# Two costs in a list scheduler: a longer tail for accumulating DMAs, a longer hop between engines

## The chip, the cores and the metric

The kernel runs on one core of a Trainium2 chip. The core has five engines that work through their own instruction queues in fixed order and meet only at semaphores: TensorE (PE, matmuls), VectorE (DVE), ScalarE (ACT), GpSimd (POOL, here memsets and four DMAs) and SyncE (SP, which issues the loads and stores). The metric is the device time of one execution in microseconds (us). A profile is one execution taken by the hardware profiler; its rows give starts and lengths in us from the start of the span.

## The reference

The reference is the joint network of a speech model. Inputs are bf16; B = 2, T = 4000, D = 512, K = 5 taps, U = 8.

```python
xp = jnp.pad(x, ((0,0),(pad,pad),(0,0)))
h = sum of einsum("btc,cd->btd", xp[:, i:i+T, :], w1[i]) over the 5 taps
h = gelu(h)[:, ::2, :]                      # (2, 2000, 512)
f = the same with hp = pad(h) and w2
f = gelu(f)[:, ::2, :]                      # (2, 1000, 512)
fe = einsum("btd,de->bte", f, w_f)
ge = einsum("bud,de->bue", g, w_g)
j = tanh(fe[:, :, None, :] + ge[:, None, :, :])
return einsum("btud,dv->btuv", j, w_o)      # (2, 1000, 8, 512)
```

So there are two convolutions of stride 2, a projection, a tanh over every pair of time and label, and a last matmul over 16000 rows.

## The kernel before, in words

**Layout.** Channels lie on the partitions, 512 channels as 4 blocks of 128: `k` numbers the blocks of a product's input, `m` those of its output. The program's batch 0 is `x[1]`, and its batch 1 is `x[0]`.

**Convolutions.** A convolution of stride 2 is done with fewer products than taps: sums and differences of inputs (on VectorE) are multiplied with sums and differences of weights (VectorE and ScalarE), and the results are recombined. Batch 0's first convolution runs in three tiles of columns (`Tile_`, L628), two of 252 columns per phase and one of 498. For each tile and each `m`, `stages` gives five pieces: `one` and `two` (products, a copy to `cs` on ScalarE, a subtraction `acc<-cs,acc` on VectorE), then `end0` and `end1`, eight matmuls each, followed by a gelu on ScalarE into `hT` (L650). The second convolution of batch 0 and both of batch 1 use `Triple` (L705), which makes three output phases from six input phases. `prepare(k0, k1)` builds its operands on VectorE from `hT` or `zx`: float32 intermediates `q` in `r32b` or `r32` (operations of 336 columns a block, 672 for two blocks), the operands `t0`, `ti`, `t1`, `tm`, `s1`, `sm` in `wide` or `row`, and `s0`, `si`, `t2` in place. `stages` then does the products, with copies to `sd` on ScalarE. For batch 0, `prepare` is called for input blocks 0 and 1 together, then for block 2, then for block 3; the products of `s1` and `t1` over blocks 0 to 2 stand ahead of those over block 3 (`split`, L770). A `tail_zero` memset on VectorE (L994, shown at L996) comes before each `prepare` and waits for the gelus that write the blocks concerned.

**Weights for the second convolution.** `w2sums` (L598) builds sums and differences. `w2quads` (L610) needs `4*w2[4] + 2*w2[2] + w2[0]` and lets DMAs add: ScalarE writes `4*w2[4]` as float32 into `half` (two buffers, `half0` and `half1`, each for two output blocks) and `2*w2[2]` into `w2_t[1]`, POOL issues two accumulating DMAs for each half (`acc`, L589, issue at L590), and ScalarE converts `half` back into `w2_t[1]` with a scale of 1/3. That last conversion, `w_t<-half`, waits for the second accumulation.

```python
act(v, w2_sb[4, :, sl], ACT.Copy, scale=4.0)
act(t, w2_sb[2, :, sl], ACT.Copy, scale=2.0)
acc(v, w2_sb[0, :, sl])
acc(v, t)
act(t, v, ACT.Copy, scale=1.0 / 3.0)
```

`w1extra` (L619) builds further first-layer weights for batch 1 by four `quad` calls: two multiplies on VectorE through the buffers `ws32_0` to `ws32_3` (shown as `ws`) and a copy on ScalarE (`w_sb<-ws`).

**Loads.** SP loads the first weights and inputs, then the second layer's weights. The six transposing loads of `zx0` (batch 1's input) have a dependency on the last accumulating DMA (`load_z`, L469).

**Joint part.** `fe` (L972) projects batch 0, with twelve copies to `feT` on VectorE or ScalarE. `tanh` (L983) writes `jT` in rings of 2048 columns for each `k`. `joint_tile` (L1007) multiplies 128 rows with `wo_sb`, evacuates the bank to `ost` on VectorE or ScalarE, and SP stores it. The 125 tiles are placed between batch 1's convolutions, and the rest follow at the end.

**What sets the order.** Nothing runs when it is written down. All calls make entries in a `Plan` (L67), with a cost each. `edges` (L100) finds the dependencies. `schedule` (L144) computes a latest start for each entry backwards and runs `simulate` (L190) up to 16 times; each time `urge` (L172) makes the entries before TensorE's gaps more urgent, and the order with the shortest simulated end is kept. In `simulate`, TensorE and SP take the first ready entry in program order; ScalarE, VectorE and POOL take the one with the earliest latest start. A dependency that needs a semaphore adds `HOP`; a DMA issued by POOL ends by a formula for a queue with a bandwidth and a fixed tail. Up to `pl.pin = ()` some engines are pinned to program order (all four until `pl.pin = ("pe",)`, then TensorE alone). `emit` (L236) writes each engine's queue in the order found, with the semaphore waits.

Of the kernel before, what the change touches and what calls it, by code (L numbers as in the profile page):

```python
# [66 lines left out]
class Plan:  # L67


    COMPUTE = ("pe", "act", "dve", "pool")  # L70
    HOP = 0.16
    ROUNDS = 16

    def __init__(self, nc):
# [69 lines left out]
    def schedule(self, pred):  # L144


        ops, HOP = self.ops, self.HOP
        n = len(ops)
# [5 lines left out]
        for i in range(n - 1, -1, -1):  # L154
            o = ops[i]
            span = o.cost + ((8.0 if o.eng == "pool" else 4.0) if o.dma else 0.0)
            t = min([late[s] - (HOP if pred[s][i] else o.cost - span) for s in succ[i]], default=0.0)
            if o.eng == "pe":
# [31 lines left out]
    def simulate(self, pred, succ, late):  # L190


        ops, HOP = self.ops, self.HOP
        n = len(ops)
        left = [len(p) for p in pred]
        ready = [0.0] * n
        free = {e: 0.0 for e in ("pe", "act", "dve", "pool", "sp")}
        cand = {e: [] for e in free}
        for i in range(n):
            if not left[i]:  # L200
                cand[ops[i].eng].append(i)
        order = {e: [] for e in free}
        wire, soft, start = 0.0, 0.0, [0.0] * n
        for _ in range(n):
            best = None
            for e, c in cand.items():
                if c:
                    t = max(free[e], min([ready[i] for i in c]))
                    if best is None or t < best[0]:
                        best = (t, e)  # L210
            t, e = best
            now = [i for i in cand[e] if ready[i] <= t + 0.02]
            i = min(now) if e in ("pe", "sp") else min(now, key=lambda i: (late[i], i))
            cand[e].remove(i)
            order[e].append(i)
            o = ops[i]
            start[i] = t
            free[e] = t + o.cost
            end = free[e]
            if o.dma and e == "pool":  # L220
                soft = max(soft, end + 1.0)
                busy = wire > soft + 1.0
                soft += o.nbytes / (60e3 if busy else 230e3)
                wire += o.nbytes / 220e3 if busy else 0.0
                end = max(soft, end + 2.0)
            elif o.dma:
                wire = max(wire, t + 1.3) + o.nbytes / o.rate
                end = max(wire, t + 2.0)
            for s in succ[i]:
                ready[s] = max(ready[s], end + HOP if pred[s][i] else free[e])  # L230
                left[s] -= 1
                if not left[s]:
                    cand[ops[s].eng].append(s)
        return order, start, max(free.values())
# [902 lines left out]
```

## Time and profile before

Median of 11 runs: 269.83 us (269.01 to 270.21).

| What | us |
|---|---|
| the profiled execution's own time | 269.4 |
| its span, first to last instruction | 267.6 |
| TensorE busy in the span | 259.8 (97%) |
| VectorE busy | 201.1 (75%) |
| ScalarE busy | 181.1 (68%) |
| POOL busy | 6.9 (3%) |
| TensorE idle before its first matmul (1.19) and waiting for `wide` (1.74) and `jT` (0.70) | 3.6 |
| first matmul of the second convolution of batch 0 | starts at 59.20 |
| first matmul of a joint tile | starts at 90.29 |

The granted TensorE clock is 1.0 of full speed over the span. A timeline row reads: start, length, engine, line, operation, output and input tiles, shapes, how many, and in brackets how long the engine stood idle before and what ended it. Several rows of one kind in succession are merged, and consecutive operations of an engine overlap by some 0.08 to 0.1 us, so that the step from start to start is a little less than the length. Rows of a helper carry the helper's line (L404 and L585 on VectorE, L409 on ScalarE, L417 on TensorE); the tile names tell them apart. The chain of waits follows the work that ended last back to the start.

### The profile page before, as it was taken

What the parts mean: (1) busy time and instruction counts of PE and PEld (TensorE: products, weight loads), DVE (VectorE), ACT (ScalarE), POOL (GpSimd) and SP (SyncE); (2) the same over time, 40 slices, a digit from 0 to 9 for tenths busy, and PEclk for the clock granted to TensorE, in tenths of its full rate; (3) what the DMA queues carried; (4) which work ended last, traced back from release to release, by engine and by line L of the source; (5) the groups of instructions that cost most, each with busy time, mean ns of one, the idle gap of its engine ahead of it and who ended that gap; (6) DMA issues with size and microseconds to landing.
All of it is one profiled execution on the core that took longest, in us unless ns stands there. A gap on an engine that the chain in (4) does not pass through costs nothing.

```text
span 267.6 us, 4331 instructions
## 1 busy us (share of the span) xinstructions
PE 259.8 (97%) x1582; PEld 151.9 (57%) x1582; DVE 201.1 (75%) x362; ACT 181.1 (68%) x302; POOL 6.9 (3%) x20
## 2 busy tenths in 40 slices
PE   8999999979999899999999999999999999999995
PEld 4897854436666555655655555565565444444442
DVE  1999999889999999994424999743255666666654
ACT  2878969684366999658448488548447695959720
POOL 1000005100000000000000000000000000000000
PEclk9999999999999999999999999999999999999999
DMA  7999998979993022111111214312101443554444
GB/s 247 319 175 211 309 236 154 161 129 191 218 178 66 13 93 72 60 40 60 43 56 42 78 40 138 120 59 78 42 20 60 148 149 118 174 178 160 154 145 132
DMA packets 56706, 33.91 MB, mean 127 GB/s; under 512 B 31582, under 2 KB 56430, under 8 KB 56686
## 3 DMA queue, kind: packets, MB, share of 16 engines
q1 hardware_dynamic: 54430, 31.49, 44.4%
q0 software_dynamic: 2112, 2.10, 4.5%
q8 instruction: 12, 0.20, 0.3%
q14 instruction: 8, 0.07, 0.1%
q10 hardware_dynamic: 144, 0.07, 0.1%
HBM read 7.86 MB, written 16.38 MB: 91 GB/s over the span
## 4 chain that ended last, share of the span: by engine, by line
PE 70%; DVE 19%; DMA 5%; issue 3%; ACT 3%; DVEq 0%; ACTq 0%
PE acc L417 70%; DMA w_sb<-in_w_dram 4%; DVE wide L404 2%; DVE r L585 2%; DVE w_t L585 2%; DVE r32b L585 2%; DVE ws L404 2%; DMA xr<-in_x_dram 1%; DVE hT L404 1%; DVE ws L585 1%; ACT jT L409 1%; DVE w_sb L404 1%; DVE feT L981 1%; DVE w_t L404 1%; DVE sd L585 1%
## 5 line engine op out<-in xcount | busy, mean ns | idle before, releaser
L417 PE MATMUL acc<-wo_sb,jT 128*128 128x512 bf16 (+1 forms) x504 | 114.9, 377 | 0.7 <-ACT jT L409 0.7
L1029 DVE CAST ost<-acc 128x512 bf16<-128x512 f32 (+1 forms) x95 | 64.9, 688 | 37.9 <-PE acc L417 36.7
L409 ACT ACTIVATE jT<-feT,geT 128x1000 bf16<-128x1000 f32 (+16 forms) x100 | 76.5, 819 | 13.4 <-PE acc L417 10.3
L417 PEld LDWEIGHTS acc<-wo_sb,jT 128*128 128x128 bf16 x504 | 49.2, 98 | 53.5 <-ACT jT L409 1.0
L409 ACT ACTIVATE ost<-acc 128x512 bf16<-128x512 f32 (+1 forms) x31 | 18.0, 582 | 15.9 <-PE acc L417 15.6
L417 PE MATMUL acc<-xt,w_sb 128*128 128x252 bf16 (+1 forms) x144 | 23.5, 305 | 0.0
L409 ACT ACTIVATE hT<-acc 128x334 bf16<-128x334 f32 (+3 forms) x33 | 15.1, 463 | 9.6 <-PE acc L417 9.5
L409 ACT ACTIVATE sd<-acc 128x334 f32<-128x334 f32 (+1 forms) x32 | 13.8, 443 | 11.0 <-PE acc L417 11.0
L417 PE MATMUL acc<-row,w_sb 128*128 128x334 bf16 (+1 forms) x112 | 20.5, 305 | 0.0
L417 PEld LDWEIGHTS acc<-xt,w_sb 128*128 128x128 bf16 x144 | 14.1, 98 | 6.7
L417 PE MATMUL acc<-zx,w_sb 128*128 128x334 bf16 (+1 forms) x96 | 17.6, 305 | 0.0
L404 DVE TENSOR_TENSOR sd<-sd 128x334 f32<-128x334 f32 (+1 forms) x16 | 8.1, 504 | 10.8 <-ACT sd L409 10.7
L417 PE MATMUL acc<-row,w_t 128*128 128x334 bf16 (+1 forms) x80 | 14.6, 305 | 0.0
L417 PEld LDWEIGHTS acc<-row,w_sb 128*128 128x128 bf16 x112 | 10.9, 98 | 6.2
L417 PE MATMUL acc<-xs,w_t 128*128 128x252 bf16 (+1 forms) x76 | 14.0, 314 | 0.3 <-ACT cs L409 0.2
L417 PE MATMUL acc<-fT,wf_sb 128*128 128x333 bf16 (+1 forms) x96 | 14.0, 305 | 0.2 <-ACT fT L409 0.2
L409 ACT ACTIVATE fT<-acc 128x334 bf16<-128x334 f32 (+1 forms) x16 | 7.1, 446 | 8.0 <-PE acc L417 7.7
L417 PEld LDWEIGHTS acc<-zx,w_sb 128*128 128x128 bf16 x96 | 9.4, 98 | 5.4
L417 PEld LDWEIGHTS acc<-fT,wf_sb 128*128 128x128 bf16 x96 | 9.3, 97 | 4.5 <-ACT fT L409 0.2
L417 PE MATMUL acc<-xs,w_sb 128*128 128x252 bf16 (+1 forms) x72 | 11.4, 293 | 0.4 <-issue 0.4
L417 PE MATMUL acc<-hT,w_t 128*128 128x334 bf16 x64 | 11.7, 305 | 0.0
L417 PE MATMUL acc<-hT,w_sb 128*128 128x334 bf16 x64 | 11.5, 305 | 0.0
(86 smaller groups left out, 318.8 us busy)
## 6 DMA issues: line engine op xcount, KB each, us to landing
out_dram<-ost SPq DMA_DIRECT2D x109, 128.0 KB, 1.9
w_sb<-in_w_dram SPq DMA_DIRECT2D x10, 512.0 KB, 5.6
xr<-in_x_dram SPq DMA_DIRECT2D x2, 512.0 KB, 4.0
half<-w_sb POOLq DMA_DIRECT2D x2, 512.0 KB, 6.6
half<-w_t POOLq DMA_DIRECT2D x2, 512.0 KB, 5.4
wf_sb<-in_w_f_dram SPq DMA_DIRECT2D x1, 512.0 KB, 7.6
wg_sb<-in_w_g_dram SPq DMA_DIRECT2D x1, 512.0 KB, 6.3
wo_sb<-in_w_o_dram SPq DMA_DIRECT2D x1, 512.0 KB, 7.1
```

Of the source, the lines that this page charges most:

```text
L404: pl.op(eng, lambda e: e.tensor_tensor(out=o.ap, in0=a.ap, in1=b.ap, op=op), (a, b), (o,), vec_cost(o, (a, b)))
L409: pl.op("act", lambda e: e.activation(o.ap, i.ap, func, scale=scale, bias=0.0 if bias is None else bias.ap), rd, (o,), cost or o.ap.free_s ...
L417: ins = e.matmul(o.ap, lhsT=l.ap, rhs=r.ap, start=start and n == 0, stop=stop and n == len(pairs) - 1, skip_group_check=not check)
L585: pl.op(eng, lambda e: e.scalar_tensor_tensor(out=o.ap, in0=a.ap, scalar=f, in1=b.ap, op0=ALU.mult, op1=op), (a, b), (o,), vec_cost(o, (a, ...
L981: pl.op("dve", lambda e, o=o, v=v: e.tensor_copy(out=o.ap, in_=v.ap), (v,), (o,), 0.47)
L1029: pl.op("dve", lambda e, o=o, v=v: e.tensor_copy(out=o.ap, in_=v.ap), (v,), (o,), vec_cost(o, (v,)))
```

## The change

`HOP`, which `schedule` and `simulate` add to a dependency across engines, becomes 0.2 where it was 0.16. In `simulate`, a DMA issued by POOL begins to move data 3.0 after its issue has ended where it was 1.0, and ends at the earliest 4.0 after the issue where it was 2.0. Nothing else in the program is altered; the operations are the same, and the planner puts them into another order. SP's and POOL's queues come out in the same order as before. On ScalarE and VectorE entries change places between 18 and 120 us of the old trace and at a few places between 150 and 170; on TensorE the products of the second convolution of batch 0 do.

```diff
@@ class Plan
-    HOP = 0.16
+    HOP = 0.2
@@ simulate
             if o.dma and e == "pool":
-                soft = max(soft, end + 1.0)
+                soft = max(soft, end + 3.0)
                 busy = wire > soft + 1.0
                 soft += o.nbytes / (60e3 if busy else 230e3)
                 wire += o.nbytes / 220e3 if busy else 0.0
-                end = max(soft, end + 2.0)
+                end = max(soft, end + 4.0)
```

ScalarE's list around the accumulated weights, before and after (hT<-acc are the gelus of the 498-column tile, b.1 its first for block b and b.2 its second):

```diff
 hT<-acc 1.1 (block 1, first)
-w_sb<-w_sb
-w_t<-half0
-hT<-acc 1.2
-w_sb<-ws
-w_t<-half1
-hT<-acc 2.1
-w_t<-w_t
-w_sb<-ws
-hT<-acc 2.2
-hT<-hT (blocks 0, 1)
-w_t<-w_t
-hT<-acc 3.1
-hT<-hT (block 2)
-hT<-acc 3.2
+w_sb<-w_sb
+w_t<-w_t
+hT<-acc 1.2
+w_sb<-ws
+w_sb<-ws
+w_t<-w_t
+w_sb<-ws
+hT<-acc 2.1
+w_t<-half0
+hT<-acc 2.2
+hT<-hT (blocks 0, 1)
+w_t<-half1
+hT<-acc 3.1
+hT<-hT (block 2)
+hT<-acc 3.2
```

## The prediction

> **What bounds the kernel now.** I read the page's totals first, then TensorE's own waits, then the chain of work in order of time, then the timelines of ScalarE, VectorE and TensorE where that chain has holes.
>
> Page, busy shares and the chain by engine:
>
> ```profile
> span 267.6 us, 4331 instructions
> PE 259.8 (97%) x1582; PEld 151.9 (57%) x1582; DVE 201.1 (75%) x362; ACT 181.1 (68%) x302; POOL 6.9 (3%) x20
> ...
> PE 70%; DVE 19%; DMA 5%; issue 3%; ACT 3%; DVEq 0%; ACTq 0%
> ```
>
> TensorE is busy for 259.8 of 267.6 us, and the change alters no matmul. All it can win is TensorE's idle time, and all it can lose is new idle time. Where that idle time lies (us in total, times, longest):
>
> ```profile
> PE acc L417 <- DVE wide L404: 1.7, 1, 1.7
> ...
> PE acc L417 <- ACT jT L409: 0.7, 1, 0.7
> ```
>
> The rest of it is the start (1.2), three pieces of 0.2 to 0.4, and the last store. The chain in order of time (start, length, what):
>
> ```profile
> 51.69 0.96 issue
> ...
> 56.46 0.76 issue
> ...
> 90.29 174.02 PE acc L417 x968
> ```
>
> From 90.29 on TensorE waits for nothing. Before that, from 36.9 to 86.9, the chain runs along VectorE, with two holes in which VectorE itself stood. ScalarE's timeline says why (start, length, instruction, idle before it):
>
> ```profile
> 51.06 1.06 ACT L409 ACTIVATE w_t<-half 128x1024 bf16<-128x1024 f32 x1 [1.68 <-DMA half<-w_t]
> 52.03 0.57 ACT L409 ACTIVATE hT<-acc 128x498 bf16<-128x498 f32 x1
> ...
> 54.13 1.06 ACT L409 ACTIVATE w_t<-half 128x1024 bf16<-128x1024 f32 x1 [1.01 <-DMA half<-w_t]
> 55.09 0.57 ACT L409 ACTIVATE hT<-acc 128x498 bf16<-128x498 f32 x1
> ...
> 56.59 0.58 ACT L409 ACTIVATE hT<-acc 128x498 bf16<-128x498 f32 x1
> ```
>
> ScalarE reached the two conversions of the accumulated weights (half0, half1) before the accumulating DMAs had landed, and stood 1.68 and 1.01 us. The gelus (hT<-acc) queued behind. A gelu can start 0.20 after its products end (block 0's second gelu: products to 43.86, start 44.06). Block 1's second one was ready at 49.95 and ran at 52.03; block 2's second was ready at 54.15 and ran at 56.59. VectorE's preparation of the second convolution waits for exactly these two, first in its memsets:
>
> ```profile
> 52.64 0.68 DVE L585 SCALAR_TENSOR_TENSOR ws<-w_sb 128x512 f32<-128x512 bf16 x1 [0.97 <-DVE acc L404]
> ...
> 57.22 0.84 DVE L404 TENSOR_TENSOR wide<-r32b 128x668 bf16<-128x668 f32 x1 [0.76 <-issue]
> ```
>
> TensorE then comes to the end of the first convolution with nothing prepared:
>
> ```profile
> 56.46 1.00 PE L417 MATMUL acc<-xt,w_sb 128*128 128x498 bf16 x4
> 59.20 0.60 PE L417 MATMUL acc<-wide,w_t 128*128 128x334 bf16 x3 [1.74 <-DVE wide L404]
> ```
>
> **The change part by part.** It changes two costs in the planner; what the chip sees is the new order in each queue, which I read from the instruction lists of both kernels. No compute instruction or DMA is added or removed. POOL's queue and SP's queue keep their order. The steps:
>
> *1. ScalarE, 38 to 58 us.* The conversion of half0 moves behind block 2's first gelu, that of half1 behind block 2's second; three copies of the extra first-layer weights fill the space. Walk with lengths from the rows (gelu 0.46, weight copy 0.52, conversion 0.97, copy of 668 columns 0.65, each start to start): block 1's second gelu 49.95 to 50.4, copies to 52.0, a fourth copy to 52.8, block 2's first gelu (ready 52.45) to 53.2, half0 to 54.2, block 2's second gelu (ready 54.15) to 54.7, the hT copy to 55.3, half1 to 56.3, block 3's first gelu to 56.8, its second (ready 57.5) to 58.1. The accumulations landed by 51.06 and 54.13; the reads now stand at 53.2 and 55.3, so 2.1 and 1.2 us are in hand. Queued behind these reads are block 2's second and block 3's first gelu; the latter is 0.5 late, and VectorE comes to its memset for block 3 only at 59.1. The use of the converted weights is at 66.01 in the old trace (hT,w_t matmuls), far behind.
>
> *2. VectorE, 51 to 64 us.* The memset that waited to 52.60 now needs a gelu that ends at 50.4; VectorE is there at 51.6 (last acc at 51.00, 0.60 long). The weight multiply in this place is another one of the same 0.60. So the first 672-column operation starts at 52.25 where it started at 53.24: 0.99 won. Two of these at 0.77, then 0.41, 0.77, 0.42: 55.4. The memset for block 2 needs the gelu of 54.7: no hole, 0.76 won. Then 0.76 to 56.15, and the planner has put the 334-column sum (wide<-hT, 0.24) for block 2 ahead of its two 0.42 operations: it is ready at 56.4. Further 0.42, 0.42, 0.24, 0.42: the t1 operand at 57.9; then 0.42, 0.77, three of 0.42, 0.24 and 0.42: block 3's two operands at 60.6 and 61.0 (before: 62.0 and 62.4). VectorE is 0.99 + 0.76 = 1.75 ahead.
>
> *3. TensorE, 57 to 64 us.* It ends the first convolution at 57.30 and finds s1 of blocks 0 to 2 there (56.4). Its list now takes s1 for two output blocks (2 x 0.43) ahead of t1, needed at 58.15, there at 57.9. At 60.7 it needs block 3's s1 (60.6), at 61.13 t1 (61.0). These are tight; with a copy of the finished sums to sd that now starts 0.28 later relative to the matmuls I allow up to 0.3 of new waits. TensorE is 1.6 to 1.9 ahead from here.
>
> *4. From 64 to 90.29.* VectorE is busy without a hole here, and the swaps (one r32 operation before the sd pair of block 3, one zx operation before the first feT copy, the same operations in each sum up to the feT copy at 84.63) do not lengthen its queue before that copy. The tanhs follow: at 85.26 ScalarE starts on them and is busy to 90.2, in the same list but for one 0.41 tanh ahead of a feT copy. So the first joint tile's tanh comes 1.75 earlier. TensorE arrives 1.6 to 1.9 earlier and still waits 0.5 to 0.8 there, as now 0.70.
>
> *5. The zx loads.* SP starts them when the last accumulation lands (54.16 in the old trace); POOL's order is kept, and the half0 copy on ScalarE moves ahead of one gelu (up to 0.8 earlier), so they do not come later. Each issue takes 1.75; the third ends at 59.4, landing took at most 9.3, so at most 68.7, and VectorE wants them at 73.95 - 1.75 = 72.2. Hidden; with that cover gone each us of lateness would cost one.
>
> *6. The first 25 us.* A copy to tc moves behind a long shift on ScalarE (1.77), so the copy to cs, for which TensorE waited 0.19 at 24.74, comes 0.27 earlier; on VectorE one 0.60 operation passes another. Bounds: -0.33 (both small holes there gone) to +0.60 (one operation late); I take 0, nearest to the swap of equals.
>
> *7. After 90.29.* Swaps of evacuations with zx, row and jT operations, and one 0.60 weight multiply of block 3 that was done at 52.64 and is now done near 112, against another that left 95.03. The trace shows no TensorE wait here, so it does not show how much slack there is. Bounds: 0 to one VectorE operation (0.77) at each of two or three places; I take 0, since the idle time of ScalarE before its evacuations (15.6 us in 13 waits) and VectorE's (36.7 in 68) says that evacuation mostly waits for TensorE, not the reverse.
>
> Sum: -1.75. The profiled execution took 269.4 (span 267.6 and 1.8 around it), which gives 267.65; it lies 0.43 under the median of 269.83, so the forecast against the median is **268.1**.
>
> A rule that speaks against step 1: the accumulating DMA issued by POOL at 45.15 was seen as landed at 51.06 (5.9 us), the one at 49.26 at 54.13 (4.9). The Trainium skill, "DMA: Bandwidth & Descriptors", section "Anatomy of one DMA — SWDGE (gpsimd) path", puts such a transfer at about 2.0 us plus bytes / 436e3, an estimate of 3.2 us for 512 KB. By that figure the third would land at 48.35, before ScalarE stands free at 49.38, and later reads would win nothing there (269.8 in all). The row decides against the rule.
>
> **The rivals.** (a) *Given back at the first joint tile*: if tanh does not move with VectorE, the wait at 90.29 grows from 0.70 by what was won, and the time is 269.8. For it: TensorE waits there now. Against: the chain leads from that wait through feT copies into VectorE's gapless queue. (b) *Half of it*: the accumulations land later in the new order, or block 3's operands come late; one of the two holes stays (0.99 or 0.76), 268.9. (c) *More*: the wait for jT goes too, and the small ones: 1.74 + 0.70 + 0.16 = 2.6, 267.2. Against: both ends of it move alike. (d) *Slower*: between 91 and 121 VectorE is full, and the new list puts zx (0.41), r32 (0.77), row (0.77) and the 0.60 multiply ahead of evacuations whose banks TensorE takes next. Together 2.55 if none has slack: 269.83 - 1.75 + 2.55 = 270.6. It decides from 1.75 of them on. Against: TensorE never waited for a bank there, and in the same stretch one 0.60 operation is gone. (e) *The planner did not do what its costs say*: excluded by the lists, where both reads have moved.
>
> **How the numbers follow.** A difference under 0.2% (0.54 us) can't be told from none. Forecast near 268.1 (0.3 either way): 0.62. (b): 0.13. (c): 0.09. (a): 0.08. (d): 0.08. Faster by over 0.2%: 0.62 + 0.13 + 0.09 = 0.84; same 0.08; slower 0.08. The range takes in (c) at its lower end, and above (b) one further operation of 0.5: 267.2 to 269.4; what it leaves out is (a) and (d), 0.16.
>
> **What would show it.** Right: the conversions of half without idle time for a DMA; block 2's second gelu near 54.2; VectorE's first 672-column operation near 52.2, no hole at 56; TensorE's 1.7 wait for wide gone or under 0.4; the first jT matmul near 88.5, then none idle. Wrong: conversions still waiting; an unchanged time of the first joint tile (a); TensorE idle between 90 and 125 for an evacuation or sd (d).

## The result and the profile after

The changed kernel took 267.75 us (median; 267.33 to 268.20), beside 269.45 us for the kernel before on the same chip (median; 268.58 to 270.39). The ratio, which is that of the mean times, is 0.9935, with a 95% interval of 0.9925 to 0.9946: faster by 0.65%, or 1.75 us (the medians differ by 1.70). The forecast was 268.1 us against the earlier median of 269.83, a ratio of 0.9936. Beside the experiments the changed kernel was run once more, on a chip with the kernel before at 269.77: 267.77 us, ratio 0.9924 [0.9906, 0.9941].

The profiled execution took 267.66 us; its span is 265.9 where it was 267.6. The page's totals and the chain's shares by engine:

```profile
span 265.9 us, 4332 instructions
PE 260.4 (98%) x1582; PEld 151.7 (57%) x1582; DVE 201.0 (76%) x362; ACT 181.3 (68%) x302; POOL 6.8 (3%) x20
...
PE 80%; DVE 14%; ACT 3%; issue 2%; DVEq 0%; ACTq 0%
```

The engines do the same work as before; what is gone is idle time of TensorE. The chain's shares do not show the change: the DMA's 5% before were the first loads, between 0.7 and 14.0 us, in whose place the chain now follows TensorE's own work. TensorE's own waits (us in total, times, longest) no longer hold the 1.7 for `wide`:

```profile
PE acc L417 <- DVE zero L424: 1.2, 1, 1.2
PE acc L417 <- ACT jT L409: 0.5, 1, 0.5
PE acc L417 <- issue: 0.3, 1, 0.3
PE acc L417 <- ACT fT L409: 0.2, 1, 0.2
```

ScalarE's timeline (start, length, instruction) where the accumulated weights are read. Neither conversion has a bracket for a DMA behind it any more, and the gelus at 52.99 and 54.40 (block 2's two) stand around the first one instead of behind both:

```profile
52.99 0.57 ACT L409 ACTIVATE hT<-acc 128x498 bf16<-128x498 f32 x1
53.45 1.05 ACT L409 ACTIVATE w_t<-half 128x1024 bf16<-128x1024 f32 x1
54.40 0.58 ACT L409 ACTIVATE hT<-acc 128x498 bf16<-128x498 f32 x1
...
55.51 1.06 ACT L409 ACTIVATE w_t<-half 128x1024 bf16<-128x1024 f32 x1
56.46 0.58 ACT L409 ACTIVATE hT<-acc 128x498 bf16<-128x498 f32 x1
```

VectorE's timeline: both holes (0.97 and 0.76) are filled. The first 672-column operation starts at 52.34 where it started at 53.24, and the sum that started at 57.22 starts at 55.48 without idle time:

```profile
52.34 1.61 DVE L585 SCALAR_TENSOR_TENSOR r32b<-hT 128x672 f32<-128x672 bf16 x2
...
55.48 0.84 DVE L404 TENSOR_TENSOR wide<-r32b 128x668 bf16<-128x668 f32 x1
```

TensorE's timeline: the first products on `wide` follow the last ones of the first convolution at once, and the first joint tile comes at 88.55 (before: 90.29). From there the chain of waits has one line, as it had before, of the same length:

```profile
56.70 1.00 PE L417 MATMUL acc<-xt,w_sb 128*128 128x498 bf16 x4
57.54 1.01 PE L417 MATMUL acc<-wide,w_t 128*128 128x334 bf16 x6
...
88.55 1.90 PE L417 MATMUL acc<-wo_sb,jT 128*128 128x512 bf16 x8 [0.47 <-ACT jT L409]
```

```profile
88.55 174.02 PE acc L417 x968
```

**A ruler for all runs.** Profiles of one kernel differ by some tenths before 30 us, so spans alone do not compare orders well. I cut each profile's span in three by two starts on TensorE's timeline, and show that profile's S, A and R beside the times of all runs: S is the start of the first 498-column matmul (the third tile of the first convolution); A goes from there to the first `fT` matmul, and holds the whole stretch around the accumulated weights; R is the rest. S + A + R is the span, which the page gives to 0.1, so R holds to about 0.05.

| Kernel | time, us | ratio to before [95%] | S | A | R |
|---|---|---|---|---|---|
| before | 269.45 | 1 | 29.91 | 50.42 | 187.27 |
| after | 267.75 | 0.9935 [0.9925, 0.9946] | 30.15 | 48.67 | 187.08 |
| after, again | 267.77 | 0.9924 [0.9906, 0.9941] | 30.06 | 48.67 | 187.07 |
| 1: two conversions moved | 268.65 | 0.9959 [0.9946, 0.9971] | 30.39 | 49.12 | 187.39 |
| 2: two conversions moved back | 268.28 | 0.9946 [0.9927, 0.9964] | 30.29 | 49.27 | 187.04 |
| 3: tail alone | 268.13 | 0.9942 [0.9919, 0.9964] | 29.94 | 48.56 | 187.30 |
| 4: hop alone | 268.58 | 0.9959 [0.9943, 0.9976] | 30.30 | 49.27 | 186.93 |
| 5: no second accumulation | 268.33 | 0.9940 [0.9918, 0.9962] | 30.68 | 48.56 | 187.26 |
| 6: orders of TensorE and VectorE alone | 269.81 | 0.9997 [0.9986, 1.0007] | 30.58 | 50.42 | 187.10 |
| 7: half copies earlier | 267.85 | 0.9931 [0.9915, 0.9948] | 30.78 | 48.56 | 187.26 |
| 8: tail of 5 | 268.04 | 0.9928 [0.9910, 0.9945] | 29.82 | 48.67 | 187.01 |
| 9: short tanhs first, on after | 267.95 | 0.9924 [0.9912, 0.9936] | 29.93 | 48.66 | 187.11 |
| 10: the same, on the tail alone | 267.92 | 0.9932 [0.9914, 0.9949] | 29.88 | 48.56 | 187.36 |
| 11: and two more tanhs, on after | 268.26 | 0.9942 [0.9922, 0.9962] | 30.72 | 48.67 | 187.11 |

### The profile page after: what moved, and what is told of

Read it like the earlier page. It is cut to its first block, busy times and chain, and to the rows that moved or that the text cites. A ratio compares the mean times of both kernels' runs of the same rounds, so it can differ in the third digit from the quotient of the medians.

```text
span 265.9 us, 4332 instructions
## 1 busy us (share of the span) xinstructions
PE 260.4 (98%) x1582; PEld 151.7 (57%) x1582; DVE 201.0 (76%) x362; ACT 181.3 (68%) x302; POOL 6.8 (3%) x20
## 4 chain that ended last, share of the span: by engine, by line
PE 80%; DVE 14%; ACT 3%; issue 2%; DVEq 0%; ACTq 0%
PE acc L417 79%; DVE wide L404 2%; DVE r L585 2%; DVE r32b L585 2%; ACT w_t L409 1%; DVE ws L585 1%; DVE hT L404 1%; ACT jT L409 1%; DVE feT L981 1%; PE acc L510 1%; DVE sd L585 1%; DVE wide L734 1%; DVE row L585 1%; DVE row L734 1%; DVE acc L585 1%
```

## The experiments

Theory A, the prediction's: ScalarE reaches the conversions before the accumulating DMAs have landed and stands; the gelus queued behind are late, and through them VectorE and TensorE. Theory B: the conversions' wait is only where it shows, and the gain comes from the order of other work, above all TensorE's `s1` ahead of `t1` and VectorE's early sum for block 2. The diffs are lists of instructions in shortened form, ScalarE's unless said otherwise; g2.1 is block 2's first gelu. "Counted from S" means less that profile's S.

**1 and 2. The two conversions alone, forwards and back.** In the order of before, only the two conversions move:

```diff
 g1.1
-w_t<-half0
 g1.2
 w_sb<-ws
-w_t<-half1
 g2.1
+w_t<-half0
 w_t<-w_t
 w_sb<-ws
 g2.2
+w_t<-half1
```

> The order of before, with two entries of ScalarE's queue moved and nothing else: the conversion of half0 goes behind block 2's first gelu, that of half1 behind block 2's second. Theory A (ScalarE's queue stood for the accumulating DMAs, and the gelus behind it held VectorE): VectorE's holes of 0.97 and 0.76 go, TensorE's wait for wide falls from 1.74 to under 0.3, ratio to before 0.9925 to 0.9950, some 267.5 to 268.1 us. Theory B (the won time comes from the other moves: s1 of two output blocks ahead of t1 on TensorE, the block 2 sum ahead of its 336-column operations on VectorE): none of these is made here, so 0.998 to 1.002.

Measured: 0.9959 [0.9946, 0.9971], between the two ranges: less than theory A gave, more than theory B. ScalarE has no DMA wait left, and the list of TensorE's waits names no matmul that waited for `wide` (two of its weight loads still do, 0.8 together): A falls from 50.42 to 49.12, by 1.30 of the 1.75 that the change wins there. Something is still late, and ScalarE's and VectorE's timelines name it:

```profile
53.43 1.05 ACT L409 ACTIVATE w_t<-half 128x1024 bf16<-128x1024 f32 x1
54.37 0.62 ACT L409 ACTIVATE w_t<-w_t 128x512 bf16<-128x512 bf16 x1
54.89 0.62 ACT L409 ACTIVATE w_sb<-ws 128x512 bf16<-128x512 f32 x1
55.41 0.57 ACT L409 ACTIVATE hT<-acc 128x498 bf16<-128x498 f32 x1
```

```profile
59.46 0.85 DVE L585 SCALAR_TENSOR_TENSOR r32b<-hT 128x672 f32<-128x672 bf16 x1 [0.43 <-issue]
```

g2.2 runs at 55.41, behind two weight copies that the changed kernel does earlier, in the time ScalarE used to stand; g3.2 and VectorE's operation on block 3 are late in the same way. So in this order the place of the conversions is the larger part. That the copies pulled into the gap are the rest of it is argued from these rows; the copies alone were not moved.

The other way round, the order of after with the two conversions put back ahead of the gelus:

```diff
 w_t<-w_t
+w_t<-half0
 g1.2
 w_sb<-ws
 w_sb<-ws
 w_t<-w_t
 w_sb<-ws
+w_t<-half1
 g2.1
-w_t<-half0
 g2.2
 hT<-hT
-w_t<-half1
```

> The order of after, with the same two conversions moved back ahead of the gelus they stood ahead of (half0 ahead of block 1's second, half1 ahead of block 2's first). Theory A: ScalarE waits for the accumulations again, 1.2 to 1.7 and 0.7 to 1.2 us, VectorE's holes return, and most of 1.7 us is given back, less up to 0.5 for the moves that stay: ratio to before 0.997 to 1.001. Theory B: the won time stays, ratio 0.993 to 0.995.

Measured: 0.9946 [0.9927, 0.9964], so theory A's number was missed and B's was hit. The reason is on ScalarE's timeline, where the conversions stand in the old places and still do not wait, and on POOL's, where the last two accumulations are issued 0.5 and 0.8 earlier than before (45.15 and 49.26), or 0.9 and 1.2 counted from S:

```profile
50.33 1.06 ACT L409 ACTIVATE w_t<-half 128x1024 bf16<-128x1024 f32 x1
51.29 0.57 ACT L409 ACTIVATE hT<-acc 128x498 bf16<-128x498 f32 x1
...
53.84 1.04 ACT L409 ACTIVATE w_t<-half 128x1024 bf16<-128x1024 f32 x1
54.78 1.05 ACT L409 ACTIVATE hT<-acc 128x498 bf16<-128x498 f32 x2
```

```profile
44.65 1.27 POOL L590 DMA_DIRECT2D half<-w_t  x1 [2.59 <-ACT w_t L409]
48.47 1.28 POOL L590 DMA_DIRECT2D half<-w_t  x1 [2.55 <-DMA half<-w_sb]
```

The rest of after's order had covered the wait already: ScalarE makes the two `half` copies one gelu earlier, and it has one more weight copy ahead of the first conversion than before, and three more ahead of the second. What moving back costs is 0.60 in A (49.27 against 48.67). VectorE's timeline shows where. Its memset at 51.98, which waits for block 1's second gelu, comes no later than in after (21.69 in both, counted from S). The weight multiply behind it waits for ScalarE's copy `w_sb<-ws`, which now stands behind the first conversion:

```profile
52.48 0.69 DVE L585 SCALAR_TENSOR_TENSOR ws<-w_sb,ws 128x512 f32<-128x512 bf16 x1 [0.43 <-ACT w_sb L409]
```

The first 672-column operation then comes 0.61 later than in after, counted from S. So work behind a conversion can be held in other ways than through the gelus. This run could not tell A from B, since both old DMA waits were gone; 3, 5 and 7 do.

**3 and 4. The two constants apart.** The tail alone, with the hop at 0.16; and the hop alone, with the old tail.

```diff
 # 3
     HOP = 0.16
-                soft = max(soft, end + 1.0)
+                soft = max(soft, end + 3.0)
-                end = max(soft, end + 2.0)
+                end = max(soft, end + 4.0)
```

> Only the tail of the accumulating DMAs is longer (3.0 and 4.0), the hop stays at 0.16. TensorE's order comes out as before; ScalarE's conversions move behind the gelus. Theory A: all of it, ratio 0.992 to 0.995, with TensorE's wait for wide under 0.3. Theory B: TensorE's order is as before and the block 2 sum stays behind its operations, so 0.998 to 1.002.

Measured: 0.9942 [0.9919, 0.9964]. TensorE's list is that of before, `s1` and `t1` in the old order, and yet there is no wait for `wide`; the conversions are read without waiting:

```profile
53.49 1.05 ACT L409 ACTIVATE w_t<-half 128x1024 bf16<-128x1024 f32 x1
54.44 0.58 ACT L409 ACTIVATE hT<-acc 128x498 bf16<-128x498 f32 x1
...
55.55 1.05 ACT L409 ACTIVATE w_t<-half 128x1024 bf16<-128x1024 f32 x1
```

A is 48.56, the least of all. TensorE's swap and VectorE's early sum are not needed for the gain in A.

```diff
 # 4
-    HOP = 0.16
+    HOP = 0.2
```

> Only the hop is longer (0.2), the tail as before. Both conversions stay ahead of block 1's second and block 2's first gelu; s1 is moved ahead as in the whole change, and other entries move. Theory A: ScalarE still waits 1.0 to 1.7 twice, VectorE keeps its holes, ratio 0.997 to 1.003. Theory B: ratio 0.993 to 0.996.

Measured: 0.9959 [0.9943, 0.9976]; A's expectation of no change was missed, and B's range was hit. The conversions keep their places and still wait, 1.02 and 0.98 in place of 1.68 and 1.01, but they start at 50.29 and 53.32 where they started at 51.06 and 54.13:

```profile
50.29 1.06 ACT L409 ACTIVATE w_t<-half 128x1024 bf16<-128x1024 f32 x1 [1.02 <-DMA half<-w_t]
51.25 0.57 ACT L409 ACTIVATE hT<-acc 128x498 bf16<-128x498 f32 x1
...
53.32 1.06 ACT L409 ACTIVATE w_t<-half 128x1024 bf16<-128x1024 f32 x1 [0.98 <-DMA half<-w_t]
```

The accumulations are issued at 44.67 and 48.45, as in 2. Counted from S, the conversions start 1.16 and 1.20 earlier than before. So the hop has another road to a gain of 1.15 in A: it does not read the sums later, it makes them earlier. VectorE's and TensorE's lists change in this kernel too (VectorE's first hole is filled with another multiply, its second is still 0.66), so how much of the 1.15 is due to the earlier sums alone is not separated here. The hop wins 0.34 more in R. The two constants' gains overlap and do not add: 1.86 and 1.15 apart, 1.75 together.

**5. The landing without the order.** The order of before on every engine, less two DMAs:

```diff
             acc(v, w2_sb[0, :, sl])
-            acc(v, t)
             act(t, v, ACT.Copy, scale=1.0 / 3.0)
```

> The order of before on every engine, with the second accumulating DMA of each half left out (the two that add 2*w2[2]), so that the sum of weights lacks that term; ScalarE's conversion of half0 then waits for a sum issued at about 39.8 us and landed near 45, that of half1 for one landed near 49, both ahead of their turns at 49.4 and about 51.5. Theory A (the late landing is the cause: ScalarE stands 1.7 and 1.0 us at the conversions, its gelus and through them VectorE and TensorE come late): no idle for a DMA ahead of the conversions, first gelu of block 2 at 53 to 54 where it began at 55.09, TensorE's wait for wide under 0.5 us where it was 1.74, ratio 0.992 to 0.997. Theory B (the order in which the pieces of work stand is what costs; the DMA's wait is only seen there): order unchanged, so ratio 0.999 to 1.001 and the wait for wide still 1.2 or more.

Measured: 0.9940 [0.9918, 0.9962]. With the sums there in time, the old order has no wait at the conversions, and the gelus follow them at 51.01 and 53.23:

```profile
50.06 1.05 ACT L409 ACTIVATE w_t<-half 128x1024 bf16<-128x1024 f32 x1
51.01 0.58 ACT L409 ACTIVATE hT<-acc 128x498 bf16<-128x498 f32 x1
...
51.99 1.06 ACT L409 ACTIVATE w_t<-half 128x1024 bf16<-128x1024 f32 x1
53.23 0.59 ACT L409 ACTIVATE hT<-acc 128x498 bf16<-128x498 f32 x1 [0.18 <-PE acc L417]
```

A is 48.56, as with the tail alone. Theory B, which wanted no change here, falls. This kernel also lets SP start the `zx` loads sooner (49.68), but VectorE takes them at 72.86 without idle time, as in all kernels here, and in 3, where the loads start at 54.26, A is the same.

**6. The other order without the landing.** ScalarE's list of before, with the lists of TensorE and VectorE that the changed planner makes:

```diff
 (in words)
-order = old plan on every engine
+order = old plan on ScalarE, new plan on TensorE and VectorE
```

> TensorE's and VectorE's orders are those of after, ScalarE's order is that of before, conversions and half copies in their old places. Theory A: ScalarE still stands about 1.7 and 1.0 us at the two conversions, so the gelus of blocks 1 and 2 keep their times within 0.4 us; products of s1 put ahead of t1 can shorten TensorE's wait for wide by some of 1.74 us, but the products and the fT evacuations behind them come no earlier, so ratio 0.997 to 1.002. Theory B: the orders of TensorE and VectorE carry the gain, ratio 0.993 to 0.996.

Measured: 0.9997 [0.9986, 1.0007], nothing. ScalarE stands at the conversions (1.13 and 1.01), and TensorE waits in two pieces, 0.70 and 0.47, where it waited 1.74 in one. The first `wide` product comes a little sooner and the next ones later, and A is 50.42, the same as before to the hundredth:

```profile
51.54 1.06 ACT L409 ACTIVATE w_t<-half 128x1024 bf16<-128x1024 f32 x1 [1.13 <-DMA half<-w_t]
...
54.60 1.06 ACT L409 ACTIVATE w_t<-half 128x1024 bf16<-128x1024 f32 x1 [1.01 <-DMA half<-w_t]
```

```profile
58.83 1.02 PE L417 MATMUL acc<-wide,w_t 128*128 128x334 bf16 x6 [0.70 <-DVE wide L404]
60.33 1.02 PE L417 MATMUL acc<-wide,w_sb 128*128 128x334 bf16 x6 [0.47 <-DVE wide L734]
```

VectorE's new list does not suit ScalarE's old one. Its memset waits for a gelu, as theory A has it, and then its multiply waits for a ScalarE copy that stands later in the old list:

```profile
53.16 0.07 DVE L996 MEMSET hT<- 128x8 bf16 x1 [0.48 <-ACT hT L409]
53.69 0.69 DVE L585 SCALAR_TENSOR_TENSOR ws<-w_sb,ws 128x512 f32<-128x512 bf16 x1 [0.46 <-ACT w_sb L409]
```

So the two lists of after bring nothing while ScalarE keeps its own. That they would bring nothing without this added wait is not shown; that they are not needed, 3, 5 and 7 show.

**7. Two copies, two places up.** If lateness against ScalarE's turn is all, it should do to make the sums sooner. In the order of before, only the two `half` copies move, into idle time that ScalarE had at 36.2 (1.11 us):

```diff
 cs<-acc
 cs<-acc
+half0<-w_sb
+half1<-w_sb
 hT<-acc (252 columns)
 hT<-acc (252 columns)
-half0<-w_sb
-half1<-w_sb
 cs<-acc
```

> The order of before; only ScalarE's two half copies go ahead of the two gelus of t1's last block that stood before them (ScalarE stood idle 1.11 us there), so that POOL's accumulations may be issued 0.5 to 2 us earlier; the conversions keep their places. Theory A (lateness of the sums against ScalarE's turn): the idle for a DMA at the two conversions (1.68 and 1.01 us) shrinks by what the issues gain, the wait for wide falls by as much, ratio 0.993 to 0.998; if the copies now wait for their weights and hold the two gelus, up to 1.001. Theory B (places in the queue behind 48 us): ratio 0.999 to 1.001.

Measured: 0.9931 [0.9915, 0.9948], as much as the whole change, at the better end of what theory A gave. This execution ran 0.87 late already at S, by which its times have to be read: the last two issues at 44.48 and 47.28 are 1.5 and 2.9 us sooner than before, and neither conversion waits.

```profile
44.48 1.27 POOL L590 DMA_DIRECT2D half<-w_t  x1 [2.56 <-ACT w_t L409]
47.28 1.28 POOL L590 DMA_DIRECT2D half<-w_t  x1 [1.53 <-DMA half<-w_sb]
```

```profile
50.28 1.06 ACT L409 ACTIVATE w_t<-half 128x1024 bf16<-128x1024 f32 x1
51.25 0.57 ACT L409 ACTIVATE hT<-acc 128x498 bf16<-128x498 f32 x1
...
52.31 1.06 ACT L409 ACTIVATE w_t<-half 128x1024 bf16<-128x1024 f32 x1
```

A is 48.56 again. So three kernels that take the wait away in three different ways (3 reads later, 5 adds less, 7 starts sooner) end at the same A. Counted from S, each matmul of A starts within 0.03 at the same time in all three, and the kernel before falls behind them in one step of 1.87, at its first `wide` product. In 5 and 7 the lists of TensorE and VectorE are those of before. That settles theory A for the stretch A: what is won there comes from the meeting of the landing with ScalarE's turn, from whichever side.

**8. More of the tail.** 5 and 6 us in place of 3 and 4:

```diff
-                soft = max(soft, end + 3.0)
+                soft = max(soft, end + 5.0)
-                end = max(soft, end + 4.0)
+                end = max(soft, end + 6.0)
```

> The planner of after with a tail of 5 and 6 us in place of 3 and 4: the conversions move further back, behind the gelus of block 3, and TensorE puts all four s1 products ahead of t1. Theory A: nothing was left waiting for the sums in after, so no more is won in ScalarE's queue: ratio 0.992 to 0.996; if the converted weights or the sums for block 3 now come late for TensorE, 0.996 to 1.000.

Measured: 0.9928 [0.9910, 0.9945], the same as after. The conversions are read at 56.22 and 58.27, and A stays at 48.67.

**9 to 11. Is the 0.47 us at the first joint tile the next gain?** On the order of after, the long tanh pieces of k = 0 go behind the short ones, and VectorE's last two `feT` copies ahead of a row operation:

```diff
 # ScalarE
 feT<-acc
-jT0 488 columns
-jT0 1000 columns
 feT<-acc
 jT1, jT2, jT1, jT3 256 columns
 sd, row, jT2, jT3 256 columns
+jT0 488 columns
 sd, jT1, jT2, jT3 488 columns
+jT0 1000 columns
```

```diff
 # VectorE
 feT<-acc
+feT<-acc
+feT<-acc
 row<-r
-feT<-acc
-feT<-acc
```

> The order of after, and between 84 and 90 us ScalarE's two long tanh pieces of k = 0 (488 and 1000 columns, 1.70 us from start to end) go behind the 256-column pieces of all four k, and VectorE's last two feT copies go ahead of the row operation of 0.83 us. If TensorE's last wait ahead of the first joint tile (0.47 us) is the one left to win after the change: the wait for jT falls under 0.1 us, first jT matmul near 88.1, ratio 0.990 to 0.993 (267.1 to 267.6 us). If something else then ends last there (row or zx operands for the matmuls behind the joint tile), the same 0.47 us shows up as another wait behind it and the ratio stays at 0.9925 to 0.9946.

Measured: 0.9924 [0.9912, 0.9936], not told apart from after. The wait did go from where it was, and came back one step behind, since the second pieces of k = 2 and 3 now stood behind a row copy that waits 0.75 for VectorE:

```profile
87.91 1.67 PE L417 MATMUL acc<-wo_sb,jT 128*128 128x512 bf16 x7
90.12 0.73 PE L417 MATMUL acc<-zx,w_b 128*128 128x334 bf16 x4 [0.54 <-ACT jT L409]
```

The same moves on the tail alone (edit as above, on 3):

> The same two moves on the order that the longer tail gives alone (hop 0.16), where the wait for jT was 0.94 us. If that wait is what kept the tail alone from beating the change: wait for jT under 0.2 us, first jT matmul near 87.9, ratio 0.989 to 0.9925 (266.9 to 267.6 us). If the operands behind the joint tile are next, 0.993 to 0.995.

Measured: 0.9932 [0.9914, 0.9949], with 0.76 at the same second place and R no shorter than in 3. The 0.94 that this run started from is too long: the profile of 3 has a record of only seven of the first eight joint matmuls (x7, 0.22 each, and the product behind them follows at once), so the first one's record is missing, and the wait there is some 0.7, as before. The same record is missing in the profiles of 9 and 10, whose first joint matmul begins some 0.2 ahead of the row shown.

Then those two pieces as well, ahead of the `sd` and row copies, on after:

```diff
 jT1, jT3 256 columns
+jT2, jT3 256 columns
 sd<-acc
 row<-r
-jT2, jT3 256 columns
```

> The order of after with the two moves of the kernel that put the short tanh pieces first, and one more: ScalarE's second 256-column pieces of k = 2 and k = 3 go ahead of its sd and row copies (the row copy waits 0.75 us for VectorE, and in that kernel the two tanh pieces stood behind it). If the wait of 0.54 us behind the first two joint tiles was that, it goes, the matmuls behind them begin near 89.6 us, and the ratio is 0.989 to 0.992 (266.8 to 267.6 us). If something third ends last there, the ratio stays at 0.992 to 0.994.

Measured: 0.9942 [0.9922, 0.9962], just above the second range. Now it is the `sd` copy, put behind the tanhs, that is late for the bank:

```profile
88.49 1.89 PE L417 MATMUL acc<-wo_sb,jT 128*128 128x512 bf16 x8
90.92 0.73 PE L417 MATMUL acc<-zx,w_b 128*128 128x334 bf16 x4 [0.54 <-ACT sd L409]
```

R is 187.11 in 9 and in 11, 187.08 in after. By these waits, three chains (tanh, row, `sd`) through ScalarE end within about half a microsecond of each other there, and putting one ahead makes the next the last. No kernel here beats the changed one by more than its interval.

The changed kernel once more, beside 8 and 11:

> The changed kernel itself, beside the others on the same chip: ratio 0.9925 to 0.9946 as measured before; first jT matmul at 88.4 to 88.7 us with a wait of about 0.5 us.

Measured: 0.9924 [0.9906, 0.9941]; first joint tile at 88.47 with a wait of 0.48.

## Why the prediction was right

**The sum.** It said 1.75 less, out of VectorE's two holes of 0.99 and 0.76. A is 1.75 shorter in both profiles of the changed kernel, and the ratio amounts to 1.75 us. The mechanism is the forecast one; that the numbers agree to the hundredth is luck. The vanished wait is worth 1.86 in A (3, 5 and 7), of which after gives back 0.11, and beside A there are two small terms that cancel in the profiled execution: R is 0.19 shorter, S 0.24 longer.

**Step 1, ScalarE.** The walk gave starts for each instruction. The gelus and conversions predicted at 52.8, 53.2, 54.2, 55.3 and 56.3 ran at 52.99, 53.45, 54.40, 55.51 and 56.46: 0.16 to 0.25 late, about the 0.24 by which this execution was late at S. The cause is shown by 3, 5 and 7. The step was one-sided, though, in telling the gain by the move of the conversions and the gelus behind them alone. Moving the conversions alone gives 1.30 in A (1), and undoing only that costs 0.60 (2), because the earlier `half` copies and the filling of the gap do a part which either can do without the other. The prediction had the `half0` copy's earlier place, but used it in step 5 only, for the loads. It also left out that VectorE's multiply ahead of the first 672-column operation needs a ScalarE copy, and is held when that copy is late (2 and 6); in after the copy is in time.

**The rule against it.** By the Trainium skill, "DMA: Bandwidth & Descriptors", section "Anatomy of one DMA — SWDGE (gpsimd) path", the estimate for such a transfer was 3.2 us and nothing was to be won. The runs agree with the row, not with the rule: from issue on POOL to the conversion that it released there were 5.6 and 4.9 us in 4 (44.67 to 50.29, 48.45 to 53.32), 5.8 and 4.9 in 6, and 5.9 and 4.9 before.

**Step 2, VectorE.** No hole; the first 672-column operation at 52.34 (predicted 52.25). Block 2's `t1` is done by 57.98 (57.9), block 3's two operands by 60.68 and 61.10 (60.6 and 61.0), each by the start of the operation behind it.

**Step 3, TensorE.** Up to 0.3 of new waits were allowed. They are 0.11: A is 48.67 in after against 48.56 in 3, 5 and 7. The trace shows one wait, where the prediction looked for it, at the copy to `sd`. The weight load for the product at 62.22 waits for that copy, and the product starts 0.28 behind the one ahead of it, where the others of the row start 0.14 apart:

```profile
62.21 2.10 PEld L417 LDWEIGHTS acc<-wide,w_t 128*128 128x128 bf16 x16 [0.32 <-ACT sd L409]
```

Of TensorE's swap the prediction expected no gain, and 3, 5 and 7 have all of A without it.

**Step 4, up to 90.29.** The first joint tile comes 1.74 earlier, at 88.55 (predicted near 88.5). The wait left there is 0.47, just under the 0.5 to 0.8 foreseen; the orders made with the hop of 0.2 have R 186.93 to 187.11, those with 0.16 have 187.26 to 187.39, so the orders made with the longer hop win about 0.2 to 0.3 there. They do so in 6 too, where ScalarE's list is that of before. That is the part of rival (c) that came true, a fifth of a microsecond, which the sum had left out.

**Step 5, the loads.** SP starts them at 53.27 (before: 54.16), and VectorE's operations on `zx` follow at 72.22 without idle time.

**Step 6, the first 25 us.** Taken as 0, with bounds of -0.33 and +0.60. S is 0.15 and 0.24 later in the two profiles of after. It cannot be told from the spread of S between executions (last section), so the value stays open.

**Step 7, after 90.29.** Taken as 0. 174.02 us from the first joint tile to the end in both kernels, no wait in it: rival (d) had no place. Rival (a) fell with the first joint tile's time, and (b) with both holes gone.

## What to carry to other kernels

An in-order engine that reads what an asynchronous transfer delivers pays for the difference between landing and turn, and everything queued behind pays with it; the read may come later, the transfer start sooner or the gap be filled, and here these remedies overlapped, so that their gains could not be added. When a queue shows such a wait, look first for the cheapest end: here two copies moved up by two places won as much as a new order of three engines' queues. Before chasing the next small wait, see how many other chains end within the same half microsecond; here there seem to be three, and each move only changed the name of the wait.

## What the runs showed that I had not expected

**The start is not repeatable, and it stays in the time.** Kernels 1, 5 and 7 have the instruction lists of before on every engine up to S. S was 29.91 before and 30.39, 30.68 and 30.78 in these, a spread of 0.87 us. These were on different chips, but "after, again" and 11 were on one chip, with the same lists up to S, and lie 0.66 apart (30.06 and 30.72). Nothing later gives it back: A and R are the same to 0.1 us whatever S was (3, 5 and 7: A 48.56 three times, R 187.26 to 187.30). In 1, TensorE's waits list 0.4 and 0.3 us for the first loads; in 5 and 7 the difference is not traced to a row. So one span compares two orders to no better than some 0.3%, while A compares to hundredths and R to about a tenth.

**In A, the accumulations cost nothing but the wait.** Taking two accumulating DMAs away altogether (5) won no more in A than reading them later (3) or starting them sooner (7), although each of them takes some 5 us.
